# A retention layer and two expert layers on one core: decay masks made by scans instead of copied by transfers

## The chip, the cores and the metric

One Trainium2 chip, one core of it. The metric is the device time of one execution in microseconds (us): 525.28 us before the change, the median of three runs (523.79 to 527.53).

## The reference, cut to what matters

The program has three parts. The first is a retention layer ("attention" below) over q, k, v of shape 2 x 8 heads x 768 positions x 64, with one decay lam per head:

```python
Dmask = np.where(rel >= 0, lam[:, None, None] ** rel[None, :, :], 0.0)   # rel = i - j
intra = np.einsum('bhic,bhjc->bhij', qb, kb) * Dmask[None]
inter = np.einsum('bhid,bhde->bhie', qb * lam_pow[None], kv_state)       # lam_pow = lam ** (i + 1)
kb_dec = kb * rev_pow[None]                                              # rev_pow = lam ** (block - 1 - j)
kv_state = lam_block * kv_state + np.einsum('bhsd,bhse->bhde', kb_dec, vb)
```

The second part maps its 1536 x 512 result x to `((x @ w1) * (x @ w2)) @ w3 @ w_out`. The third sends each of the 1536 rows to one of 8 experts (argmax of `x @ w_gate`, at most 384 rows for each expert, in order of rows), computes `relu(x @ w1[e]) @ w2[e]` and scales it by the softmax weight. Results are float32.

## The kernel before, in words

**Stages, in order of time.** Attention (0 to 72 us), the product of w3 and w_out (72 to about 121 us), the gate stage with w1 and w2 and the ranking of rows, then the experts. Products of float32 accuracy are made from high and low parts (`whi`, `wlo`, `xth`, `xtl`) with three matmuls each (L295 to L297).

**Attention** runs over `it` 0 to 7, each one pair of heads of one batch (`pair = it // 2`), in blocks of 128 positions (`NC` = 6) where the reference has 64, which gives the same result. `part1(it)`: GpSimd scales the queries (`qs`, L394); TensorE makes the scores (24 matmuls, L408); VectorE multiplies them with the mask (`at`, L417, four instructions); TensorE makes the keys-by-values of the blocks from decayed keys `kd` (20 matmuls, L430); VectorE carries the state along the blocks with one scan (`state`, L438). `part2(it - 1)` follows in the same iteration: L454 (24 matmuls) and L468 (20), ScalarE and VectorE split the output (L477, L478). Then ScalarE makes `kd` for the next iteration (`decay_keys`, L379).

**Masks before.** VectorE makes powers of lam by doubling (L334, L337) in `tab`, whose row for a head is 127 zeros, a one, and the powers. ScalarE copies the powers to `lp`. A mask of 128 x 128 is copied from one row of `tab`, each partition reading 128 elements that start one element later (`load_mask`, L356, two transfers of 64 KB for each pair, on the SP queue). That order of partitions reverses positions in a block, so the host reverses keys and values in blocks. TensorE turns powers into a column (`kcol`, L372) that scales the keys.

**Loads.** The SP queue issues in program order: `tqk` and `tkv` of an iteration (L306, L308), then staged weights (`st`, L122). `tqk` has two buffers, `tkv` three; `load_qkv(it + 2)` stands at the end of iteration `it`, so an issue waits until its buffer's readers are through, and what is behind it on the queue waits too. Weights w_out and w3 come in chunks of 512 KB as 64-bit floats; a piece of one is turned to float32 by ScalarE (L132, L133, L142), VectorE (L135, L138) and GpSimd (L143). `TICKS` says where in an iteration a piece begins: one in `it` 1, two in each later one, the second at its end. Chunks 0 to 7 are w_out, chunk 8 and on w3; a staging buffer comes free when the chunk four places earlier has been read by VectorE.

**Keeping TensorE running.** `keep_warm(n)` issues n matmuls on zeros (L325): `WARM` = 15 at the start, `KW` = (7, 6) in iteration 0 after the scores and after the keys-by-values.

```python
def keep_warm(count):
    for _ in range(count):
        nc.tensor.matmul(wacc, warm[:, 0:P], warm, start=True, stop=True)
```

Of the kernel before, what the change touches and what calls it, by code (L numbers as in the profile page):

```python
# [8 lines left out]
F32 = mybir.dt.float32  # L9
F32R = mybir.dt.float32r  # L10
F16 = mybir.dt.float16
# [17 lines left out]
BIG = 1 << 20  # L29
WARM = 15  # L30
KW = (7, 6)
NST = 4
# [8 lines left out]
@with_exitstack  # L41
def tile_moe_chain(ctx, tc, cap, qk, kv, lamb, w12, w3i, woi, wgi, e1i, e2i, c32, c16, zero, out):
    nc = tc.nc
# [20 lines left out]
    def bank():  # L64
        return ps.tile([P, 512], F32, tag="b", name="bank")
# [138 lines left out]
    def run_bg(n=1):  # L204
        for _ in range(n):
            feed.tick()
# [62 lines left out]

    c32_sb = const.tile([P, 156], F32, name="c32_sb")  # L270
    c16_sb = const.tile([P, 256 + ntab], F16, name="c16_sb")
# [4 lines left out]
    utri = c16_sb[:, 0:128]  # L276
    ones = c16_sb[:, 128:256]
    iota = c16_sb[:, 256 : 256 + ntab]
    csum = const.tile([P, NE], F16, name="csum")
# [20 lines left out]
    with pool("att", 2, side="right") as ap, pool("att1", side="right") as a1:  # L300
# [3 lines left out]
        def load_qkv(it):  # L304
            tqk = ap.tile([P, 2, S], F32, tag="qk", name="tqk")
            nc.sync.dma_start(tqk, qk[it])  # L306
            tkv = ap.tile([P, 2, NC, P], F32, tag="kv", name="tkv", bufs=3)
            nc.sync.dma_start(tkv, kv[it])  # L308
            loads[it] = (tqk, tkv)

        tab = ring.tile([P, 2080], F32, tag="1l", name="tab")[:, 0:1024]
        tab = tab.rearrange("p (a n) -> p a n", n=256)
        lp = a1.tile([P, 4, P], F32, name="lp")
        decay = a1.tile([P, 2, (NC - 1) * 64], F32, name="decay")
        lam_sb = a1.tile([P, 4], F32, name="lam_sb")
# [10 lines left out]

        keep_warm(WARM)
        nc.vector.memset(wg_sb, 0.0)
        nc.gpsimd.memset(tab[:, :, 0:127], 0.0)
        nc.gpsimd.memset(tab[:, :, 127:128], 1.0)  # L330
        nc.gpsimd.memset(decay, 0.0)
        states = [a1.tile([P, (NC - 1) * 64], F32, name=f"state{n}") for n in range(2)]
        pw = tab[:, :, 128:256]
        nc.vector.tensor_copy(pw[:, :, 0:1], lam_sb.rearrange("p (a b) -> p a b", b=1))  # L334
        n = 1
        while n < P:
            nc.vector.tensor_tensor(  # L337
                pw[:, :, n : 2 * n],
                pw[:, :, 0:n],
                pw[:, :, n - 1 : n].to_broadcast([P, 4, n]),  # L340
                op=ALU.mult,
            )
            n *= 2
        nc.scalar.copy(lp, pw)

        def set_decay(pair):
            r = lp[:, pair, 127:128]
# [19 lines left out]
        kcol = a1.tile([P, 2, 4], F32, name="kcol")  # L367
        for h in range(2):
            kp = bank()[:, 0:4]
            for k in range(4):  # L370
                row = tab[h * 64 : h * 64 + 1, k, 127:255]
                nc.tensor.matmul(kp[:, k : k + 1], row, row[:, 0:1], start=True, stop=True)  # L372
            nc.vector.tensor_copy(kcol[:, h, :], kp)
# [14 lines left out]
        def part1(it, ticks):  # L388
            pair = it // 2
            if it % 2 == 0:  # L390
# [5 lines left out]
                tqk[:, 0, :].rearrange("p (c i) -> p c i", i=P),  # L396
                bass.AP(lp.tensor, lp[:, pair, :].offset, [lp[:, pair, :].ap[0], [0, NC], [1, P]]),
                op=ALU.mult,
# [3 lines left out]
            for half in range(2):  # L402
                sc = [bank(), bank()]
                for c in range(3):
                    cc = half * 3 + c
                    for h in range(2):
                        hs = slice(h * 64, h * 64 + 64)
                        nc.tensor.matmul(  # L408
                            sc[h][:, c * P : (c + 1) * P],
                            tqk[hs, 1, cc * P : (cc + 1) * P],  # L410
                            tqk[hs, 0, cc * P : (cc + 1) * P],
                            start=True,
                            stop=True,
                        )
                for h in range(2):
                    m = dmask[:, 2 * pair + h, :]
# [68 lines left out]
        for it in range(8):  # L485
# [75 lines left out]
    p2 = late.enter_context(pool("p2", 2, side="right"))  # L561
    enabled.update(w12_it)
    gts = {}
    tabs = psi.tile([P, 512], F32, tag="i", name="tabs")[:, 0 : nch * NE]
# [439 lines left out]
```

## Time and profile before

| | before |
|---|---|
| median of three runs | 525.28 us |
| the profiled execution's own time | 528.52 us |
| its span in the profile | 526.7 us |
| TensorE, matmuls busy | 507.0 us (96%) |
| VectorE busy | 263.5 us (50%) |
| ScalarE busy | 243.7 us (46%) |
| GpSimd busy | 129.4 us (25%) |
| bytes moved by transfers | 81.28 MB, mean 154 GB/s |

PE is TensorE's matmul side, PEld its weight loads, DVE VectorE, ACT ScalarE, POOL GpSimd, SP the engine whose queue issues most transfers; a q behind a name is that engine's sequencer. Shares of the whole span mix the stages: in the first 58 us the transfer engines are busy nearly all the time, after that they are not. TensorE's matmuls are pipelined, so that a busy stretch is not one at its peak.

### The profile page before, as it was taken

What the parts mean: (1) busy time and instruction counts of PE and PEld (TensorE: products, weight loads), DVE (VectorE), ACT (ScalarE), POOL (GpSimd) and SP (SyncE); (2) the same over time, 40 slices, a digit from 0 to 9 for tenths busy, and PEclk for the clock granted to TensorE, in tenths of its full rate; (3) what the DMA queues carried; (4) which work ended last, traced back from release to release, by engine and by line L of the source; (5) the groups of instructions that cost most, each with busy time, mean ns of one, the idle gap of its engine ahead of it and who ended that gap; (6) DMA issues with size and microseconds to landing.
All of it is one profiled execution on the core that took longest, in us unless ns stands there. A gap on an engine that the chain in (4) does not pass through costs nothing. (4 is left out here: it accounts for less than half of the span.)

```text
span 526.7 us, 9643 instructions
## 1 busy us (share of the span) xinstructions
PE 507.0 (96%) x3833; PEld 473.8 (90%) x3833; DVE 263.5 (50%) x572; ACT 243.7 (46%) x487; POOL 129.4 (25%) x126
## 2 busy tenths in 40 slices
PE   9889799999999999999999999899999999999994
PEld 4778699999899999999999999889898998989893
DVE  3597757565643222322233364476574747466420
ACT  2488569676831122112211342367574646466410
POOL 2255436443511000000002003603333240400101
PEclk9999899999999999999999999999999999999998
DMA  7999637555582000000010033557856666674300
GB/s 240 392 369 359 221 120 249 195 184 175 183 284 84 31 0 1 32 30 1 1 42 21 1 119 112 182 190 250 296 182 208 219 221 211 221 240 153 117 1 34
DMA packets 26210, 81.28 MB, mean 154 GB/s; under 512 B 4426, under 2 KB 7372, under 8 KB 26160
## 3 DMA queue, kind: packets, MB, share of 16 engines
q1 hardware_dynamic: 20128, 70.79, 39.2%
q0 software_dynamic: 3344, 7.85, 4.7%
q10 hardware_dynamic: 2688, 1.97, 1.1%
q8 instruction: 32, 0.52, 0.4%
q14 instruction: 18, 0.15, 0.1%
HBM read 74.78 MB, written 10.54 MB: 162 GB/s over the span
## 5 line engine op out<-in xcount | busy, mean ns | idle before, releaser
L97 DVE TENSOR_TENSOR wlo<-st,whi 128x512 fp32r<-128x512 f32 x128 | 82.0, 685 | 15.2 <-ACT whi L95 15.2
L295 PE MATMUL bank<-xtl,whi 128*128 128x384 f32 x256 | 87.2, 341 | 1.1 <-DVE t L138 1.1
L297 PE MATMUL bank<-xth,wlo 128*128 128x384 f32 x256 | 86.4, 338 | 0.0
L296 PE MATMUL bank<-xth,whi 128*128 128x384 f32 x256 | 85.9, 336 | 0.0
L95 ACT CAST whi<-st 128x512 fp32r<-128x512 f32 x128 | 72.9, 621 | 16.7 <-PE bank L297 9.4
L800 PE MATMUL bank<-xdl,whi 128*128 128x256 f32 x256 | 72.6, 284 | 2.2 <-issue 1.7
L800 PE MATMUL bank<-xdh,wlo 128*128 128x256 f32 x256 | 72.1, 282 | 0.0
L800 PE MATMUL bank<-xdh,whi 128*128 128x256 f32 x256 | 72.0, 281 | 0.0
L143 POOL TENSOR_TENSOR wlo<-t,whi 128x512 fp32r<-128x512 f32 x40 | 51.8, 1296 | 67.1 <-ACT whi L142 51.5
L295 PE MATMUL bank<-wxl,gh 128*128 128x264 f32 (+1 forms) x192 | 55.9, 291 | 0.0
L296 PE MATMUL bank<-wxh,gh 128*128 128x264 f32 (+1 forms) x192 | 54.1, 282 | 0.0
L297 PE MATMUL bank<-wxh,gl 128*128 128x264 f32 (+1 forms) x192 | 54.1, 282 | 0.0
L579 DVE TENSOR_TENSOR a_sb<-bank,a_sb 128x384 f32<-128x384 f32 x32 | 17.8, 558 | 68.3 <-PE bank L297 64.1
L800 PEld LDWEIGHTS bank<-xdl,whi 128*128 128x128 f32 x256 | 48.4, 189 | 3.1 <-issue 2.0
L295 PE MATMUL bank<-wlo,hh 128*128 128x512 f32 x128 | 50.8, 397 | 0.0
L297 PE MATMUL bank<-whi,hl 128*128 128x512 f32 x128 | 50.3, 393 | 0.0
L296 PE MATMUL bank<-whi,hh 128*128 128x512 f32 x128 | 50.3, 393 | 0.0
L295 PEld LDWEIGHTS bank<-xtl,whi 128*128 128x128 f32 x256 | 48.1, 188 | 1.7 <-DVE t L138 1.1
L813 DVE SCALAR_TENSOR_TENSOR hl<-bank,hh 128x512 fp32r<-128x512 f32 x32 | 22.1, 691 | 53.4 <-ACT hh L812 43.8
L731 POOL DMA_INDIRECT out_dram<-y,idx x16 | 16.1, 1006 | 132.3 <-ACT y L932 113.1
L800 PEld LDWEIGHTS bank<-xdh,whi 128*128 128x128 f32 x256 | 48.3, 189 | 0.3
L800 PEld LDWEIGHTS bank<-xdh,wlo 128*128 128x128 f32 x256 | 48.3, 189 | 0.0
(114 smaller groups left out, 1018.0 us busy)
## 6 DMA issues: line engine op xcount, KB each, us to landing
st<-e1i SPq DMA_DIRECT2D x32, 512.0 KB
st<-e2i SPq DMA_DIRECT2D x32, 512.0 KB
st<-w3i SPq DMA_DIRECT2D x16, 512.0 KB
st<-w SPq DMA_DIRECT2D x16, 512.0 KB
tqk<-qk SPq DMA_DIRECT2D x8, 768.0 KB
tkv<-kv SPq DMA_DIRECT2D x8, 768.0 KB
st<-woi SPq DMA_DIRECT2D x8, 512.0 KB
out_dram<-zero SPq DMA_DIRECT2D x1, 3072.0 KB
```

The lines of the kernel that those rows point to most:

```text
L95: nc.scalar.copy(h, s)
L97: nc.vector.tensor_tensor(lo, s, h.bitcast(F32), op=ALU.subtract)
L143: nc.gpsimd.tensor_tensor(lo, t, h.bitcast(F32), op=ALU.subtract)
L295: nc.tensor.matmul(acc, wh, rl, start=first, stop=False)
L296: nc.tensor.matmul(acc, wh, rh, start=False, stop=False)
L297: nc.tensor.matmul(acc, wl, rh, start=False, stop=last)
L579: nc.vector.tensor_tensor(a_sb, accs[1], a_sb, op=ALU.mult)
L731: nc.gpsimd.indirect_dma_start(out=out, out_offset=bass.IndirectOffsetOnAxis(ap=idx[:, col : col + 1], axis=0), in_=src, in_offset=None, b ...
L800: nc.tensor.matmul(o, w[:, k, :], x[:, k, :], start=m == 0 and k == 2 and x is xl, stop=m == 1 and k == 1 and w is lo, skip_group_check=True,)
L813: nc.vector.scalar_tensor_tensor(hl, acc, 0.0, hh.bitcast(F32), op0=ALU.max, op1=ALU.subtract)
```

## The change: what it does

- Masks and powers of one pair of heads are made by VectorE with three scans of 128 x 128 (`make_pair`): two whose added operand is the identity matrix give the masks of the two heads, `mask[j, i] = lam * mask[j, i - 1] + (i == j)`, and one gives the powers. Pair 0 at the start, the next ones at the end of iterations 0, 2 and 4.
- Masks and powers are held for two pairs, not four. `tab`, `kcol`, the eight mask transfers and the reversal on the host are gone; the last column of a mask scales the keys.
- `tqk` has three buffers. Loads of iteration 1 and the first chunk are issued before anything else on SP but the constants `c32` (identity, 78 KB before, 84.5 KB now), which were loaded by ScalarE's queue in iteration 1.
- `wgi` is padded to 64 KB by the host and loaded at the end of iteration 2 (16 KB at the end of iteration 1 before, into a zeroed tile). The ranking constants `c16` are loaded in the gate stage, after gate unit (0, 3), not in iteration 4.
- `WARM` is 12 and `KW` is (0, 4).

```diff
-WARM = 15
-KW = (7, 6)
+WARM = 12
+KW = (0, 4)
...
-            tqk = ap.tile([P, 2, S], F32, tag="qk", name="tqk")
+            tqk = ap.tile([P, 2, S], F32, tag="qk", name="tqk", bufs=3)
...
-        lp = a1.tile([P, 4, P], F32, name="lp")
+        lp = a1.tile([P, 2, P], F32, name="lp")
-        dmask = a1.tile([P, NE, P], F32, name="dmask")
-        nc.sync.dma_start(lam_sb, lamb)
+        dmask = a1.tile([P, 4, P], F32, name="dmask")
+        nc.sync.dma_start(c32_sb, c32)
         load_qkv(0)
+        load_qkv(1)
+        feed.load(1)
...
-        while n < P:
-            nc.vector.tensor_tensor(
-                pw[:, :, n : 2 * n],
-                pw[:, :, 0:n],
-                pw[:, :, n - 1 : n].to_broadcast([P, 4, n]),
-                op=ALU.mult,
-            )
-            n *= 2
-        nc.scalar.copy(lp, pw)
+        def powers(out, lam, add, first):
+            nc.vector.tensor_tensor_scan(
+                out, lam.to_broadcast([P, P]), add, first, op0=ALU.mult, op1=ALU.add
+            )
+
+        def make_pair(pair):
+            for e in range(2 * pair, 2 * pair + 2):
+                powers(dmask[:, e % 4, :], lam8[:, e : e + 1], ident, 0.0)
+            none = c32_sb[:, 168:169].to_broadcast([P, P])
+            powers(lp[:, pair % 2, :], lam2[:, pair : pair + 1], none, 1.0)
+
+        make_pair(0)
...
-        def load_mask(pair):
-            for h2 in range(2):
-                r = tab[h2 * 64 : h2 * 64 + 1, pair, 0:1]
-                nc.sync.dma_start(
-                    dmask[:, 2 * pair + h2, :],
-                    bass.AP(r.tensor, r.offset, [[r.ap[0][0], 1], [1, P], [1, P]]),
-                )
-
-        load_mask(0)
-        load_qkv(1)
-        feed.load(1)
...
-                    scale=kcol[:, h, it // 2 : it // 2 + 1],
+                    scale=dmask[:, (it // 2 * 2 + h) % 4, P - 1 : P],
...
-            if it in (0, 1, 3):
-                load_mask((it + 3) // 2)
-            if it == 1:
-                nc.scalar.dma_start(c32_sb, c32)
-                nc.scalar.dma_start(wg_sb[:, :, 0:NE], wgi)
-            if it == 4:
-                nc.scalar.dma_start(c16_sb, c16)
+            if it in (0, 2, 4):
+                make_pair(it // 2 + 1)
+            if it == 2:
+                nc.scalar.dma_start(wg_sb, wgi)
...
+        if (g, fb) == (0, 3):
+            nc.scalar.dma_start(c16_sb, c16)
```

## Rows read from the trace of the kernel before

**Rows 1.** Stretches: us, busy us of each engine, TensorE's granted clock, transfer share, GB/s

```profile
2.00:58.00 56.00, 51.64 (x681) 40.21 (x679) 37.98 (x75) 30.55 (x60) 24.05 (x19) 1.00 0.98 353
7.00:13.00 6.00, 6.00 (x71) 4.33 (x70) 2.59 (x7) 1.04 (x2) 0.87 (x1) 1.00 0.89 254
14.00:24.00 10.00, 8.29 (x137) 7.16 (x138) 4.72 (x9) 4.21 (x9) 3.04 (x3) 1.00 1.03 406
24.00:36.00 12.00, 10.45 (x158) 9.20 (x156) 11.77 (x22) 9.24 (x19) 4.31 (x3) 1.00 1.00 353
36.00:48.00 12.00, 11.94 (x190) 9.93 (x189) 10.49 (x19) 11.04 (x22) 8.31 (x7) 1.00 1.00 388
62.00:68.00 6.00, 6.00 (x64) 4.63 (x62) 4.04 (x8) 3.76 (x7) 4.30 (x3) 0.50 0.52 158
72.00:160.00 88.00, 86.89 (x621) 86.27 (x620) 53.92 (x93) 61.03 (x119) 37.72 (x29) 1.00 0.62 208
```

**Rows 2.** Timeline of all engines, iteration 7: start, duration, instruction, idle before it

```profile
56.93 0.48 PE L408 MATMUL bank<-tqk 64*128 64x128 f32 x2
58.06 0.62 ACT L132 ACTIVATE bank<-st 128x512 f32<-128x512 f32 x1 [5.28 <-DMA st<-w3i]
60.26 0.95 PE L408 MATMUL bank<-tqk 64*128 64x128 f32 x12 [2.84 <-DVE xtl L478]
61.43 1.65 PE L408 MATMUL bank<-tqk 64*128 64x128 f32 x10 [0.22 <-ACT wt L220]
67.84 1.45 PE L468 MATMUL bank<-qs,state 64*64 64x128 f32 x20
...
72.02 0.39 PE L295 MATMUL bank<-wlo,whi 128*128 128x256 f32 x1
```

**Rows 3.** The same view, iteration 4

```profile
35.73 0.93 PE L408 MATMUL bank<-tqk 64*128 64x128 f32 x10 [0.65 <-ACT wt L220]
...
39.20 1.40 PE L468 MATMUL bank<-qs,state 64*64 64x128 f32 x20
```

**Rows 4.** Timeline of the SP queue: issues, start and duration

```profile
4.55 1.22 SPq L356 DMA_DIRECT2D dmask<-tab  x2
5.81 0.59 SPq L306 DMA_DIRECT2D tqk<-qk  x1
...
47.44 0.33 SPq L306 DMA_DIRECT2D tqk<-qk  x1
47.86 0.38 SPq L308 DMA_DIRECT2D tkv<-kv  x1
48.41 41.96 SPq L122 DMA_DIRECT2D st<-w3i  x15
```

**Rows 5.** Timeline of all engines, iterations 0 to 2

```profile
1.19 6.10 PE L325 MATMUL bank<-warm 128*128 128x512 f16 x15 [1.19 <-DVE warm L320]
2.40 0.17 DVE L334 COPY tab<-lam_sb 128x4 f32<-128x4 f32 x1 [1.13 <-DMA lam_sb<-lamb]
6.07 1.80 POOL L394 TENSOR_TENSOR qs<-tqk,lp 128x768 f32<-128x768 f32 x1 [0.42 <-DMA tqk<-qk]
8.68 1.61 PE L408 MATMUL bank<-tqk 64*128 64x128 f32 x24
10.22 1.69 PE L325 MATMUL bank<-warm 128*128 128x512 f16 x7
13.08 1.80 POOL L394 TENSOR_TENSOR qs<-tqk,lp 128x768 f32<-128x768 f32 x1 [5.21 <-DMA tqk<-qk]
21.62 0.56 ACT L379 ACTIVATE kd<-tkv,kcol 128x320 f32<-128x320 f32 x1 [1.57 <-DMA tkv<-kv]
23.17 1.95 DVE L417 TENSOR_TENSOR at<-bank,dmask 128x384 f32<-128x384 f32 x4 [2.54 <-DMA dmask<-tab]
```

**Rows 6.** One line's instructions (L438, then L337): durations, ns, least/median/most

```profile
L438 DVE TENSOR_TENSOR_SCAN state<-decay,bank x8: 812/816/821, 12.8 to 65.4; 128x320 f32<-128x320 f32 x8
...
L337 DVE TENSOR_TENSOR tab<-tab x7: 167/191/424, 2.6 to 4.0; 128x4 f32<-128x4 f32 x1, 128x8 f32<-128x8 f32 x1, 128x16 f32<-128x16 f32 x1, 128x32 f32<-128x32 f32 x1
```

**Rows 7.** Waits of TensorE, 72 to 160 us: total, times, longest

```profile
PE bank L295 <- DVE t L138: 1.1, 2, 0.8
```

More of the change, by code (lines that the diff above doesn't have):

```diff
@@ L41, in tile_moe_chain @@
 @with_exitstack
-def tile_moe_chain(ctx, tc, cap, qk, kv, lamb, w12, w3i, woi, wgi, e1i, e2i, c32, c16, zero, out):
+def tile_moe_chain(ctx, tc, cap, qk, kv, w12, w3i, woi, wgi, e1i, e2i, c32, c16, zero, out):
     nc = tc.nc
@@ L268, in tile_moe_chain @@
         (e1_it, e2_it)[w][2 * e + j] = it
-    c32_sb = const.tile([P, 156], F32, name="c32_sb")
-    c16_sb = const.tile([P, 256 + ntab], F16, name="c16_sb")
+    c32_sb = const.tile([P, 169], F32, name="c32_sb")
     ident = c32_sb[:, 0:128]
@@ L275, in tile_moe_chain @@
     gsum = c32_sb[:, 148:156]
-    utri = c16_sb[:, 0:128]
-    ones = c16_sb[:, 128:256]
-    iota = c16_sb[:, 256 : 256 + ntab]
+    lam2 = c32_sb[:, 156:160]
+    lam8 = c32_sb[:, 160:168]
     csum = const.tile([P, NE], F16, name="csum")
@@ L327, in tile_moe_chain @@
         keep_warm(WARM)
-        nc.vector.memset(wg_sb, 0.0)
-        nc.gpsimd.memset(tab[:, :, 0:127], 0.0)
-        nc.gpsimd.memset(tab[:, :, 127:128], 1.0)
         nc.gpsimd.memset(decay, 0.0)
         states = [a1.tile([P, (NC - 1) * 64], F32, name=f"state{n}") for n in range(2)]
-        pw = tab[:, :, 128:256]
-        nc.vector.tensor_copy(pw[:, :, 0:1], lam_sb.rearrange("p (a b) -> p a b", b=1))
-        n = 1
-        while n < P:
-            nc.vector.tensor_tensor(
-                pw[:, :, n : 2 * n],
-                pw[:, :, 0:n],
-                pw[:, :, n - 1 : n].to_broadcast([P, 4, n]),
-                op=ALU.mult,
-            )
-            n *= 2
-        nc.scalar.copy(lp, pw)
+        def powers(out, lam, add, first):
+            nc.vector.tensor_tensor_scan(
+                out, lam.to_broadcast([P, P]), add, first, op0=ALU.mult, op1=ALU.add
+            )
+        def make_pair(pair):
[4 more added lines that the diff above has]
+        make_pair(0)
         def set_decay(pair):
-            r = lp[:, pair, 127:128]
+            r = lp[:, pair % 2, 127:128]
             nc.gpsimd.tensor_copy(
@@ L351, in set_decay @@
             )
-        def load_mask(pair):
-            for h2 in range(2):
-                r = tab[h2 * 64 : h2 * 64 + 1, pair, 0:1]
-                nc.sync.dma_start(
-                    dmask[:, 2 * pair + h2, :],
-                    bass.AP(r.tensor, r.offset, [[r.ap[0][0], 1], [1, P], [1, P]]),
-                )
-        load_mask(0)
-        load_qkv(1)
-        feed.load(1)
         nc.vector.memset(csum, 0.0)
         enabled.update(wo_it + w3_it[:2])
[L367 to L373, printed above, removed]
         kds = {}
@@ L396, in part1 @@
                 tqk[:, 0, :].rearrange("p (c i) -> p c i", i=P),
-                bass.AP(lp.tensor, lp[:, pair, :].offset, [lp[:, pair, :].ap[0], [0, NC], [1, P]]),
+                bass.AP(lp.tensor, lp[:, pair % 2, :].offset, [lp.ap[0], [0, NC], [1, P]]),
                 op=ALU.mult,
@@ L415, in part1 @@
                 for h in range(2):
-                    m = dmask[:, 2 * pair + h, :]
+                    m = dmask[:, (2 * pair + h) % 4, :]
                     nc.vector.tensor_tensor(
@@ L562, in tile_moe_chain @@
     enabled.update(w12_it)
+    c16_sb = p2.tile([P, 256 + ntab], F16, name="c16_sb", bufs=1)
+    utri = c16_sb[:, 0:128]
+    ones = c16_sb[:, 128:256]
+    iota = c16_sb[:, 256 : 256 + ntab]
     gts = {}
@@ L945 @@
     q, k, v, lam = f("q"), f("k"), f("v"), f("lam")
-    def rev(a):
-        return a.reshape(2, 8, NC, P, 64)[:, :, :, ::-1].reshape(2, 8, S, 64)
     def tr(a):
@@ L954, in nat @@
         return a.reshape(2, 4, 2, NC, P, 64).transpose(1, 0, 4, 3, 2, 5).reshape(8, P, NC, P)
-    kr, vr = rev(k), rev(v)
     w1, w2, w3, wo = f("moe_w1"), f("moe_w2"), f("moe_w3"), f("moe_w_out")
@@ L967 @@
     nch = min(-(-cap // P), NBLK)
-    c32 = np.zeros((P, 156), np.float32)
+    c32 = np.zeros((P, 169), np.float32)
     c32[:, 0:128] = np.eye(P)
@@ L975 @@
     c16[:, 256:] = np.arange(nch * P)
+    c32[:, 156:160] = np.repeat(lam.reshape(4, 2).T, 64, axis=0)
+    c32[:, 160:168] = lam
+    wgi = np.zeros((P, 4, 32), np.float32)
+    wgi[:, :, 0:NE] = f("moe2_w_gate").reshape(4, P, NE).transpose(1, 0, 2)
     w1h, w2h = kfb(w1), kfb(w2)
     arrays = {
-        "qk": np.stack([tr(q), tr(kr)], 2),
-        "kv": np.stack([nat(kr), nat(vr)], 2),
-        "lamb": np.repeat(lam.reshape(4, 2).T, 64, axis=0),
+        "qk": np.stack([tr(q), tr(k)], 2),
+        "kv": np.stack([nat(k), nat(v)], 2),
         "w12": np.stack([w1h[0], w2h[0], w1h[1], w2h[1]]),
@@ L983 @@
         "woi": wo.reshape(2, 4, P, DM).transpose(0, 2, 1, 3).reshape(2, P, 2048),
-        "wgi": f("moe2_w_gate").reshape(4, P, NE).transpose(1, 0, 2),
+        "wgi": wgi,
         "e1i": np.stack([kfb(e1[e]) for e in range(NE)]),
```

3 lines of the change are left out of this document (removed).

## The prediction

> **What bounds the kernel now.** I read the stretches first, since the chain of waits starts only near the end of the span. From 2 to 58 us the transfer engines are busy 0.98 of the time [rows 1]; after that transfers have slack. From 72 us on TensorE has almost no gap (86.89 of 88 us busy to 160 us), so what the change can win lies before 72 us, and moves the later stages forward as a whole.
>
> Within attention there are three regimes. In iterations 0 to 2 data is late: the second queries are seen at 13.08 us after 5.21 us of idle GpSimd, and VectorE waits 2.54 us for a mask transfer at 23.17 us [rows 5]. From 24 to 36 us VectorE is busy 11.77 of 12 us and sets the pace; from 36 to 48 us TensorE, ScalarE and VectorE are all nearly full (11.94, 11.04, 10.49) [rows 1]. In iteration 6 data is late again: ScalarE stands 5.28 us until chunk 9 of the weights (the second of w3) lands at 58.06 us; behind it stand the output copies of part2(5), VectorE's subtraction, a PSUM bank, and TensorE, idle 2.84 us up to 60.26 us [rows 2]. TensorE's granted clock, full until then, is 0.50 from 62 to 68 us [rows 1], the lower of its two levels: what it did before it fell was to stand those 2.84 us.
>
> **The change part by part.**
>
> *Start.* Gone are the doubling chain (seven instructions of 191 ns median [rows 6]), the ScalarE copy, the column matmuls and the first mask transfers, which cannot be issued until 4.55 us and stand ahead of the second tqk on SP, issued at 5.81 us [rows 4]. Now SP issues constants, both pairs of loads and a chunk back to back. The constants take the place of lam, seen at 2.40 us [rows 5], and being 84.5 KB come some 0.5 us later, so pair 0's scans run from about 3.0 us.
>
> A scan of 128 x 128: the trace has one shape, 128x320 in 816 ns [rows 6]. In proportion to its elements it would be 0.33 us, and at most the whole 0.82 us. I take 0.40 us, near the first, as the row is mostly elements: three make 1.2 us for a pair (1.0 to 2.45). Pair 0 is ready by 4.3 us, before the first scores.
>
> From 7 to 13 us the transfers move 254 GB/s while busy 0.89, against 406 GB/s in the stretch from 14 to 24 us [rows 1]: the two masks' rows stand between large ones, and the hole is worth 6 x (1 - 254/406) = 2.2 us. At 406 GB/s the second tqk, a third transfer of 768 KB after one seen at 6.07 us [rows 5], follows two more such transfers of 1.94 us each: about 10.2 us for 13.08. Later ones gain more, for the masks and the constants are no longer among them: the third tqk about 15.5 us, its tkv about 17.4 us, where ScalarE saw it at 21.62 us [rows 5].
>
> The Trainium skill speaks against so large a gain (DMA: Bandwidth & Descriptors, "Why small descriptors are slow (HBM only)"): it holds that transfers from SBUF to SBUF, as the masks are, do not suffer from small packets and keep 78% of the link's best rate. By it a pair of masks would cost an estimated 0.4 us, the hole would be no work of theirs, and the sum below would be some 2 us smaller. The row with 254 GB/s at a share of 0.89 speaks for the masks; the measurement decides.
>
> TensorE: three of 15 warm matmuls go, at 6.10/15 = 0.41 us each, and seven of 1.69 us in all after the first scores [rows 5]; two of the six after the keys-by-values go. Twelve end at about 6.2 us, when the first tqk lands, so the scores begin at 6.4 instead of 8.68 us. Keys-by-values then wait for tkv and ScalarE until about 9.3 us; the second scores come at about 11, the third at 17.4. VectorE begins the third iteration's masks at about 18.3 instead of 23.17 us: **-4.9 us**. Bounds: -2.3 (only the first scores' lead holds) and -5.5.
>
> *Scans later.* Pair 1's stand at the end of iteration 0 on an idle VectorE: nothing. If that cover is gone, 1.2 us. Pair 2's stand at the end of iteration 2, where VectorE sets the pace: +1.2 us, behind them a weight piece and the masks of iteration 3, for which TensorE's next part2 waits. Pair 3's fall in the stretch where VectorE has 1.5 of 12 us free [rows 1]: between 0 and 1.2, I take +0.6. Together **+1.8 us** (1.0 to 4.9).
>
> *Data just in time.* With VectorE 4.9 us earlier, chunks 2 and 3 and the fourth tkv land within half a microsecond of their use: **+0.5 us** (0 to 1.5). So the middle of the stage runs about 2.6 us ahead.
>
> *Third query buffer, chunk 9.* Today the last tqk waits for its buffer until 47.44 us, the last tkv goes at 47.86 and chunk 9 at 48.41 [rows 4]. With three buffers tqk waits for nothing recent; tkv (three buffers as before) still waits for part2(4), so chunk 9 is issued at about 45. Ahead of its end lie 16 transfers of 768 KB, ten of 512 KB and 0.15 MB of constants, 18.0 MB, from 2 us on. At 406 GB/s with 1.2 us for the slow first two microseconds they end at 47.5, at 388 [rows 1] at 49.6, and are seen 1 to 3 us after that. TensorE's wait of 2.84 us is gone if chunk 9 lands by 58.06 - 2.84 - 2.6 = 52.6 us. It does, with little to spare: **-2.8 us** (0 to -2.8).
>
> *Clock.* Without that idle the clock should stay up. Price: from the last ten score matmuls to L468 it takes 67.84 - 61.43 = 6.41 us at the low level and 39.20 - 35.73 = 3.47 us at the full one [rows 2, 3]: **-2.9 us** (0 to -2.9).
>
> *Moved and dropped.* The c16 load costs one issue of ScalarE in the gate stage, where ScalarE is busy 61.03 of 88 us [rows 1] and ranking needs it much later: nothing; 0.4 us without that cover. wgi is issued an iteration later and needed some 9 us after that: nothing, or up to 1 us of TensorE if late. Eight issues of 0.6 us leave SP, which stands behind busy transfers anyway.
>
> **Sum:** -4.9 + 1.8 + 0.5 - 2.8 - 2.9 = -8.3 us. Against the profiled execution, 528.52 us (1.8 of it outside the span), that is 520.2. That execution is 3.24 us above the median, about the price of the clock's fall, and the runs do not tell whether the median one had it. If it had, 525.28 - 8.3 = 517.0; if not, the gain is 5.4 and the time 519.9. I take **518.0 us**, nearer the first.
>
> **Rivals.**
>
> *Chunk 9 still late.* If the transfers keep their mean of 353 GB/s [rows 1], the 18.0 MB end at 54.1 us, and with 1 us more chunk 9 lands at about 55. For it: 24 to 36 us shows 353 with few masks in it. Against it: 10 us at 406. All before then is swallowed; what remains is 58.06 - 55 = 3 us, with the clock falling as before: 522.3 us. The Trainium skill (DMA: Bandwidth & Descriptors, "Where 436 GB/s comes from") puts the memory limit of a core at about 358 GB/s, which would make this the case; 406 GB/s over 10 us shows more.
>
> *Gain lost behind attention.* The w3 stage lives on prepared pieces, and TensorE waits for VectorE there, though only 1.1 us in two waits [rows 7]. If preparation, not TensorE, were the limit, nothing would arrive at the end: about 525. Against it: ScalarE and VectorE have 27 and 34 us free in those 88 [rows 1], and the pieces move forward with the matmuls.
>
> *Cold start, slower.* Fifteen warm matmuls run 0.41 us apart, seven later ones 0.24 [rows 5]: the rise comes with the end of the first series. With twelve, and no fill between scores and keys-by-values, TensorE could go on at the lower level. An iteration has 5.3 us of matmuls (1.6 + 0.8 + 1.5 + 1.4), and the low level makes them 6.41/3.47 = 1.85 as long: 4.5 us each. After two such iterations the gain is gone; with three, up to about 27 us, the time is 517.0 + 13.5 = 530.5. Against it: the scores follow the twelve at once. The Trainium skill (TensorE: Matmul & The Clock Gate, "What's actually happening") says that low is the resting state and activity lifts it, which leaves this open.
>
> *It does not do what it says.* If SP is held by full transfers and not by buffers, the third query buffer moves nothing; chunk 9 then goes at about 46.5 and still lands by 52.6: inside the forecast's range.
>
> **How the numbers follow.** A change under 1% (5.25 us) can hardly be told from none here. Forecast 0.55 (518.0, its own range 514 to 520); chunk 9 late 0.20 (522.3, a quarter of it under 520.0 if the clock holds); lost behind 0.10 (525); cold start 0.07 (530.5); scans at the dear end 0.08 (-8.3 + 3.1 = -5.2: 520.1, half under 520.0). Faster: 0.55 + 0.05 + 0.04 = 0.64, less 0.02 for the forecast's own upper end: 0.62. Same: 0.31. Slower: 0.07. Low end: 517.0 less 0.8 for cheap scans, 0.6 for the larger lead and about 1.5 for the spread of runs: 514. High end: the late chunk with that spread: 524.
>
> **What would show it.** Right: masks of iteration 2 near 18.3 us; no transfer rate near 254 GB/s before 13 us; scans near 0.4 us; chunk 9 landing by 52.6 us; no TensorE gap near 2.8 us in iteration 7; granted clock 1.00 through 72 us; the first L295 near 64 us instead of 72.02 [rows 2]. Wrong: a ScalarE wait for w3 that stays, a clock of 0.50 before 30 us, or a first L295 at 64 with the span unmoved.

## The result, and the profile after

The changed kernel takes 520.76 us, the median of 12 runs (518.09 to 522.96), beside 525.70 us for the kernel before, the median of 12 runs in the same comparison (523.62 to 529.02). The ratio is 0.9902, its 95% interval 0.9877 to 0.9927: by it 0.98% less, at the edge of what the forecast called no change. In two later comparisons, each on a chip of its own, it was 0.9903 (0.9874 to 0.9933) and 0.9878 (0.9857 to 0.9900). The profiled execution takes 520.25 us, with a span of 518.4 us.

Stretches of the kernel after, the columns as in [rows 1]:

```profile
7.00:13.00 6.00, 4.31 (x66) 3.25 (x62) 4.10 (x9) 3.31 (x5) 2.60 (x3) 1.00 1.01 413
14.00:24.00 10.00, 9.10 (x156) 8.20 (x152) 8.61 (x18) 6.17 (x13) 1.83 (x1) 1.00 1.02 407
24.00:36.00 12.00, 10.30 (x168) 8.93 (x168) 10.92 (x20) 10.18 (x20) 8.04 (x7) 1.00 1.02 412
36.00:48.00 12.00, 11.49 (x172) 9.69 (x170) 10.20 (x22) 11.28 (x23) 7.21 (x7) 1.00 1.01 390
62.00:68.00 6.00, 6.00 (x53) 6.00 (x52) 4.01 (x8) 3.78 (x10) 2.15 (x3) 1.00 0.53 164
331.00:341.00 10.00, 10.00 (x64) 9.51 (x65) 6.95 (x13) 6.71 (x13) 1.16 (x1) 0.86 0.38 129
```

The hole of 254 GB/s is filled (413), and 353 GB/s from 24 to 36 us became 412; the granted clock from 62 to 68 us is 1.00 where it was 0.50 [rows 1]. The last row is new: at the start of the expert stage the clock is 0.86.

Timeline of the kernel after (start, duration, instruction, idle before it):

```profile
2.73 0.74 DVE L329 TENSOR_TENSOR_SCAN dmask<-c_sb 128x128 f32<-128x128 f32 x2 [1.59 <-DMA c_sb<-c]
3.38 0.40 DVE L329 TENSOR_TENSOR_SCAN lp<-c_sb 128x128 f32<-128x128 f32 x1
6.32 1.61 PE L385 MATMUL bank<-tqk 64*128 64x128 f32 x24
7.59 1.28 ACT L356 ACT_TABLE_LOAD   x1 [7.59 <-DMA tkv<-kv]
9.47 1.81 POOL L371 TENSOR_TENSOR qs<-tqk,lp 128x768 f32<-128x768 f32 x1 [1.99 <-DMA tqk<-qk]
9.50 1.25 PE L407 MATMUL bank<-tkv,kd 128*64 128x64 f32 x20 [1.56 <-ACT kd L356]
17.66 1.94 DVE L394 TENSOR_TENSOR at<-bank,dmask 128x384 f32<-128x384 f32 x4
23.07 0.56 ACT L356 ACTIVATE kd<-tkv,dmask 128x320 f32<-128x320 f32 x1 [0.97 <-DMA tkv<-kv]
23.25 0.40 DVE L329 TENSOR_TENSOR_SCAN lp<-c_sb 128x128 f32<-128x128 f32 x1
25.06 0.80 PE L407 MATMUL bank<-tkv,kd 128*64 128x64 f32 x20 [1.96 <-DVE t L138]
...
42.24 28.85 SPq L122 DMA_DIRECT2D st<-w3i  x11
48.69 0.66 ACT L132 ACTIVATE bank<-st 128x512 f32<-128x512 f32 x1 [0.95 <-DMA st<-w3i]
51.91 1.94 PE L385 MATMUL bank<-tqk 64*128 64x128 f32 x24
...
60.53 0.39 PE L293 MATMUL bank<-wlo,whi 128*128 128x256 f32 x1
...
318.08 0.37 ACT L629 COPY rowa<-bank 128x256 f32<-128x256 f32 x1
329.38 0.58 ACT L762 CAST xdh<-bank 128x512 fp32r<-128x512 f32 x1 [5.26 <-remote]
330.75 0.58 PE L780 MATMUL bank<-xdl,whi 128*128 128x256 f32 x1 [2.65 <-issue]
```

These rows answer to [rows 2, 4, 5]: L385 is L408 of before, L371 L394, L356 L379, L394 L417, L407 L430, L293 L295. VectorE's masks of iteration 2 begin at 17.66 us for 23.17, without a wait; chunk 9 is seen at 48.69 us for 58.06, after 0.95 us of waiting for 5.28; the last scores begin at 51.91 us for 56.93, with no gap ahead of them. The first product of w3 comes 11.5 us earlier, at 60.53 for 72.02 us. The span is only 8.3 us shorter: the gap in front of the first expert (L780) and the low clock after it give back 3.2 us. The copy of rows and the cast ahead of that gap in the kernel before, 10.07 us apart where they are now 11.30, and below them the first entry of its ScalarE:

```profile
329.66 0.37 ACT L651 COPY rowa<-bank 128x256 f32<-128x256 f32 x1
339.73 0.58 ACT L782 CAST xdh<-bank 128x512 fp32r<-128x512 f32 x1 [4.00 <-PE bank L770]
...
0.73 1.28 ACT L344 ACT_TABLE_LOAD   x1 [0.73 <-PEq L994]
```

### The profile page after: what moved, and what is told of

The parts are those of the page before. It is cut to its first block, busy times and chain, and to the rows that moved or that the text cites. A ratio compares the mean times of both kernels' runs of the same rounds, so it can differ in the third digit from the quotient of the medians.

```text
span 518.4 us, 9565 instructions
## 1 busy us (share of the span) xinstructions
PE 499.3 (96%) x3805; PEld 469.4 (91%) x3805; DVE 264.1 (51%) x573; ACT 243.0 (47%) x486; POOL 128.8 (25%) x124
## 5 line engine op out<-in xcount | busy, mean ns | idle before, releaser
L293 PE MATMUL bank<-xtl,whi 128*128 128x384 f32 x256 | 87.3, 341 | 1.4 <-DVE t L138 1.4
L295 PE MATMUL bank<-xth,wlo 128*128 128x384 f32 x256 | 86.4, 337 | 0.0
L780 PE MATMUL bank<-xdl,whi 128*128 128x256 f32 x256 | 73.3, 286 | 3.7 <-issue 2.6
L780 PE MATMUL bank<-xdh,whi 128*128 128x256 f32 x256 | 72.8, 284 | 0.0
L780 PE MATMUL bank<-xdh,wlo 128*128 128x256 f32 x256 | 72.6, 284 | 0.0
L293 PE MATMUL bank<-wxl,gh 128*128 128x264 f32 (+1 forms) x192 | 55.9, 291 | 0.0
L295 PE MATMUL bank<-wxh,gl 128*128 128x264 f32 (+1 forms) x192 | 54.1, 282 | 0.0
L780 PEld LDWEIGHTS bank<-xdl,whi 128*128 128x128 f32 x256 | 49.1, 192 | 4.6 <-issue 2.8
L557 DVE TENSOR_TENSOR a_sb<-bank,a_sb 128x384 f32<-128x384 f32 x32 | 17.8, 557 | 68.0 <-PE bank L295 63.7
L293 PE MATMUL bank<-wlo,hh 128*128 128x512 f32 x128 | 51.1, 399 | 0.0
L711 POOL DMA_INDIRECT out_dram<-y,idx x16 | 17.3, 1082 | 135.1 <-ACT y L912 100.0
L295 PE MATMUL bank<-whi,hl 128*128 128x512 f32 x128 | 50.4, 394 | 0.0
L293 PEld LDWEIGHTS bank<-xtl,whi 128*128 128x128 f32 x256 | 48.1, 188 | 2.0 <-DVE t L138 1.4
L780 PEld LDWEIGHTS bank<-xdh,whi 128*128 128x128 f32 x256 | 49.0, 191 | 0.3
L780 PEld LDWEIGHTS bank<-xdh,wlo 128*128 128x128 f32 x256 | 49.0, 192 | 0.0
```

The costliest lines, as they stand in the source:

```text
L293: nc.tensor.matmul(acc, wh, rl, start=first, stop=False)
L295: nc.tensor.matmul(acc, wl, rh, start=False, stop=last)
L557: nc.vector.tensor_tensor(a_sb, accs[1], a_sb, op=ALU.mult)
L711: nc.gpsimd.indirect_dma_start(out=out, out_offset=bass.IndirectOffsetOnAxis(ap=idx[:, col : col + 1], axis=0), in_=src, in_offset=None, b ...
L780: nc.tensor.matmul(o, w[:, k, :], x[:, k, :], start=m == 0 and k == 2 and x is xl, stop=m == 1 and k == 1 and w is lo, skip_group_check=True,)
```

## The experiments

Three sets, each on one chip of its own beside runs of the kernel before. "First product" is the start of the first w3 matmul, "rest" the span less that.

| | median us | ratio (95%) | profiled: span | first product | rest |
|---|---|---|---|---|---|
| *first chip*: before again | 525.50 | 1.0003 (0.9971 to 1.0035) | 523.5 | 68.49 | 455.0 |
| after again | 520.29 | 0.9903 (0.9874 to 0.9933) | 518.4 | 60.37 | 458.0 |
| after + row transfers | 521.85 | 0.9932 (0.9907 to 0.9957) | 520.0 | 62.64 | 457.4 |
| after, scans doubled | 525.20 | 0.9996 (0.9966 to 1.0026) | 526.2 | 68.07 | 458.1 |
| *second chip*: before + early loads | 520.83 | 0.9983 (0.9965 to 1.0001) | 517.6 | 64.11 | 453.5 |
| after, two query buffers | 517.28 | 0.9924 (0.9900 to 0.9949) | 515.2 | 61.18 | 454.0 |
| after, pair 2's scans late | 519.98 | 0.9960 (0.9928 to 0.9992) | 516.6 | 62.45 | 454.2 |
| after, three pairs early | 515.64 | 0.9877 (0.9846 to 0.9908) | 513.9 | 60.38 | 453.5 |
| *third chip*: before again | 523.26 | 1.0019 (0.9989 to 1.0049) | 519.7 | 66.11 | 453.6 |
| after again | 516.28 | 0.9878 (0.9857 to 0.9900) | 515.1 | 61.55 | 453.6 |
| three pairs early again | 515.40 | 0.9860 (0.9839 to 0.9881) | 513.8 | 60.45 | 453.4 |
| after, warm matmuls of before | 516.80 | 0.9894 (0.9873 to 0.9916) | 514.9 | 60.85 | 454.1 |

**The kernel before again, on two chips** (no edit). Does the stall in iteration 6, with the clock's fall after it, belong to every execution?

> The kernel before, unchanged, profiled once more. If the clock's fall at 61 us belongs to some executions only (theory): TensorE still idles 2 to 3 us near 57 to 60 us, but the granted clock stays 1.00 from 60 to 70 us, the first w3 product (L295) starts at about 69 instead of 72.0 us and the span is about 523.8 us. If it belongs to every execution (rival): granted clock 0.50 from 62 to 68 us again and a span of 526 to 527 us; then the median's gain of 5 us hides 3 us lost somewhere later.

> The kernel before, a third profile, beside the next three on one chip. Theory (chunk 9's landing is what varies from execution to execution): ScalarE waits 3 to 5.5 us for it again, TensorE idles 1 to 3 us in iteration 7, first w3 product 66 to 72 us; from the last row copy of the gate stage to the end of the span 196 to 197.5 us, as in the changed kernels of the same chip.

First chip: ScalarE's wait for chunk 9, the last scores, and two stretches:

```profile
55.98 0.63 ACT L132 ACTIVATE bank<-st 128x512 f32<-128x512 f32 x1 [3.72 <-DMA st<-w3i]
58.19 0.95 PE L408 MATMUL bank<-tqk 64*128 64x128 f32 x12 [1.28 <-DVE xtl L478]
...
59.00:63.00 4.00, 3.78 (x44) 2.60 (x42) 3.79 (x8) 3.40 (x7) 2.61 (x2) 0.57 0.42 120
62.00:68.00 6.00, 6.00 (x102) 5.54 (x104) 4.02 (x7) 4.94 (x10) 3.81 (x3) 0.93 0.44 149
```

Third chip, the same:

```profile
55.09 0.65 ACT L132 ACTIVATE bank<-st 128x512 f32<-128x512 f32 x1 [2.07 <-DMA st<-w3i]
57.19 1.16 PE L408 MATMUL bank<-tqk 64*128 64x128 f32 x14
...
62.00:68.00 6.00, 6.00 (x82) 5.59 (x81) 5.38 (x9) 5.80 (x12) 4.44 (x4) 1.00 0.48 135
```

Three executions of one kernel: ScalarE waits 5.28, 3.72 and 2.07 us, TensorE stands 2.84, 1.28 and 0 us, the clock from 62 to 68 us is 0.50, 0.93 and 1.00, and the first product comes at 72.02, 68.49 and 66.11 us. On the first chip the clock did fall, only earlier and for less long: it is 0.57 from 59 to 63 us. So neither expectation held as written: on the first chip the stall was shorter than the theory's 2 to 3 us and the clock fell all the same, and on the third ScalarE waited less than 3 us and TensorE not at all. The stall is real and its size is not fixed; the execution from which the prediction was made had it at its largest. What belongs to the chip and what to the single execution is not told apart by three profiles, but the twelve runs on the first chip alone lie between 522.74 and 529.57 us. The profiled run there, 525.28 us, is close to their median; the one on the third, 521.45 us, is 1.8 us under its median.

**The kernel after again, on two chips** (no edit). Do the 3 us at the experts belong to the change?

> The changed kernel, unchanged, profiled once more. Both theories: first w3 product within 0.5 us of 60.5 us, ratio to before 0.988 to 0.993. Theory (the wait where the experts begin is chance): TensorE's gap near 330 us differs from 2.65 us by 0.5 us or more and the clock there may stay full, span 516.5 to 519. Rival (the change moved a load into that place): again 2.6 us and a fall of the clock, span 518.4 within 0.5 us.

> The changed kernel, a third profile. First w3 product 60 to 61 us on any chip. If the 3 us that it lost after attention in two profiles belong to the change (rival), 200 us from the last row copy to the end and a fall of the clock near 330 us again, ratio to before 0.990; if they belong to the chip and the moment (theory), 196 to 197.5 us, and a ratio of 0.986 to 0.990.

First chip; the gap and the low clock come back:

```profile
330.79 0.58 PE L780 MATMUL bank<-xdl,whi 128*128 128x256 f32 x1 [2.60 <-issue]
...
330.00:336.00 6.00, 5.21 (x32) 5.21 (x33) 2.90 (x5) 2.78 (x7) 1.91 (x2) 0.72 0.10 30
```

Third chip:

```profile
24.00:30.00 6.00, 4.79 (x62) 4.50 (x64) 4.96 (x9) 3.75 (x8) 4.31 (x3) 0.72 1.03 411
...
319.19 0.37 ACT L629 COPY rowa<-bank 128x256 f32<-128x256 f32 x1
327.83 0.59 ACT L762 CAST xdh<-bank 128x512 fp32r<-128x512 f32 x1 [2.58 <-PE bank L750]
...
330.00:342.00 12.00, 12.00 (x77) 10.84 (x76) 9.79 (x16) 8.12 (x16) 1.62 (x2) 1.00 0.65 204
```

On the third chip TensorE has no gap there (12.00 of 12 us) and the clock stays at 1.00. From the last row copy to the first cast it takes 8.64 us; the kernel before takes 8.63 there (323.64 to 332.27 us). In the first comparison and on the first chip the same stretch takes 10.07 and 10.29 us before, 11.30 and 11.26 after. On the first chip the rival held to the letter (gap 2.60 us, span 518.4 us); the third chip decides that the 3 us are no fixed price of the change: the rest of the program is as long for both kernels on the third chip (453.6 us; 196.1 and 195.9 us from that copy to the end), and 3 us longer for the changed one on the first. That the gathers land later on the first chip, and another microsecond later in the changed kernel, is measured; why is **open**. Two things narrow it. The doubled scans below bring the first product of that chip back to 68.07 us, as late as in the kernel before, and their rest is still 458.1 us, so an earlier arrival alone does not explain it. And GpSimd stands 1.3 to 1.5 us ahead of the same gather (L701 of the kernel after) in every profile of a changed kernel with the longer rest, and 0.3 us in the others. The move of the `c16` load into the gate stage was not undone in any run. On the third chip another disturbance showed, a clock of 0.72 from 24 to 30 us, and the gain of the profiled pair is 4.6 us, in the first product and in the span alike; by the medians it is 6.3 us there.

**The masks' transfers back, without their use.** Six copies of rows, two at each place of the later masks, into a tile that nothing reads (`copy_rows`, not shown, issues two transfers of 64 KB: 128 rows of 512 bytes out of one partition). The first pair's two, in front of the loads of iteration 1, are not put back:

```diff
+            if it in (0, 1, 3):
+                copy_rows(0)
```

> The changed kernel with six transfers of 64 KB put back on the SP queue where iterations 0, 1 and 3 issued mask transfers, of the same form (each partition reads 128 elements of one row, one element further), into a tile that nobody reads. Theory (such transfers cost the engines far more than their bytes): the transfer rate shows holes as before, chunk 9's wait on ScalarE grows from 0.95 to 2.5 to 4 us, first w3 product 2 to 4 us later (62.5 to 64.5). Rival (they cost their bytes only, 0.39 MB at 406 GB/s = 1 us): first w3 product 0 to 0.7 us later.

```profile
51.59 0.66 ACT L132 ACTIVATE bank<-st 128x512 f32<-128x512 f32 x1 [2.03 <-DMA st<-w3i]
...
24.00:36.00 12.00, 9.51 (x156) 8.19 (x158) 10.21 (x19) 10.12 (x20) 7.25 (x6) 1.00 1.01 384
```

Chunk 9 is seen 2.26 us later than in the kernel after on that chip (49.33 us), the first product 2.27 us later, the median 1.56 us. From 24 to 36 us the rate is 384 GB/s for 408. The transfers hold 0.39 MB, 1.0 us at 406 GB/s; in this pair of executions they cost more than twice that, and by the medians half as much again. The forecast of 2 to 4 us for the first product held; the hole in the rate (the lowest stretch is 384 GB/s) and a wait of 2.5 us or more did not come. This is the direct measurement of six of the eight mask transfers: about three tenths of the change's gain on that chip. Whether the engines or the queue pay is not told apart, for each two issues also hold the SP queue 1.1 to 2.3 us, and chunk 9 is issued 1.0 us later (43.02 for 42.02 us).

**Scans doubled** after the first pair:

```diff
             if it in (0, 2, 4):
                 make_pair(it // 2 + 1)
+                make_pair(it // 2 + 1)
```

> The changed kernel with the three scans made twice at the end of iterations 0, 2 and 4 (1.1 us more of VectorE each time). Theory (VectorE sets the pace in iterations 2 and 3, less so in 4 and 5): first w3 product 2.0 to 2.8 us later (+1.1 after iteration 2, +0.6 after iteration 4, +0.3 to 1.1 after iteration 0). Rival (the scans lie beside other work): 0 to 0.4 us later.

```profile
11.00:14.00 3.00, 3.00 (x18) 1.84 (x18) 2.70 (x7) 1.01 (x2) 0.66 (x2) 0.51 1.02 390
...
25.31 1.75 DVE L329 TENSOR_TENSOR_SCAN dmask<-c_sb 128x128 f32<-128x128 f32 x2
25.33 1.44 POOL L143 TENSOR_TENSOR wlo<-t,whi 128x512 fp32r<-128x512 f32 x1 [4.97 <-ACT whi L142]
26.73 1.92 POOL L371 TENSOR_TENSOR qs<-tqk,lp 128x768 f32<-128x768 f32 x1
26.98 1.95 DVE L329 TENSOR_TENSOR_SCAN lp<-c_sb 128x128 f32<-128x128 f32 x1
30.34 1.34 PE L407 MATMUL bank<-tkv,kd 128*64 128x64 f32 x20 [5.49 <-issue]
...
24.00:36.00 12.00, 6.51 (x82) 5.90 (x79) 10.33 (x17) 4.71 (x10) 4.61 (x3) 0.72 0.82 316
```

The median is 4.9 us above the kernel after, more than the scans' own time: nine more of 0.40 us are 3.6 us. The profiled execution (528.01 us) is 2.8 us above that median, so its first product, 7.7 us later than the kernel after's and outside both expectations, is not the median's price. Alone a scan takes 0.40 us; beside GpSimd the second mask and the powers take 1.4 and 1.95. Each ends 0.3 us after the GpSimd instruction that began before it (26.77 and 28.65 us; the scans end at 27.06 and 28.93). TensorE then stands 5.49 us where it stood 1.96 us, and its clock, 0.72 over the stretch, adds to it. Of the 7.7 us, 1.8 are there before these scans begin: the clock is 0.51 from 11 to 14 us, after TensorE stood 2.22 us up to 9.64 us, ahead of the keys-by-values, and the scores of iteration 1 take 2.59 us for 1.61. The first extra scans begin only at 12.67 us; this start is the change's own.

The Trainium skill (SBUF — State Buffer, "SBUF: two separate sides") describes this: VectorE and GpSimd share a pair of ports as an exclusive lock, taken also by a VectorE instruction with two SBUF inputs against a GpSimd instruction that reads SBUF, and whoever starts first keeps it for the whole instruction. The trace agrees, with those two ends. In the kernel after all 12 scans take 0.40 us (the longest 0.42), since GpSimd happens to be idle beside every one.

**The early order of loads alone**, in the kernel before: the second pair of loads and the first chunk ahead of the first masks, as the change has them.

```diff
         load_qkv(0)
+        load_qkv(1)
+        feed.load(1)
...
         load_mask(0)
-        load_qkv(1)
-        feed.load(1)
```

> The kernel before with one thing of the change: loads of iteration 1 and the first chunk are issued ahead of the first mask transfers. Theory (early order needs masks that come by no transfer): the second tqk lands near 10 us instead of 13, but the first masks now stand behind 2 MB and land near 13 us, so the first mask products start 3 to 4 us later than 9.6 us; first w3 product between 67.5 and 71, ratio 0.996 to 1.003. Rival (the order alone is the gain): first w3 product 3 us or more ahead of the kernel before (65.5 or less), ratio 0.994 or less.

```profile
7.00:13.00 6.00, 6.00 (x70) 4.12 (x70) 0.33 (x2) 2.04 (x4) 2.69 (x3) 1.00 1.04 378
...
13.07 1.95 DVE L417 TENSOR_TENSOR at<-bank,dmask 128x384 f32<-128x384 f32 x4 [4.85 <-DMA dmask<-tab]
```

The masks come at 13.07 us, behind the larger transfers, and VectorE waits 4.85 us for them. By the ratio the time is 0.17% lower, in an interval that reaches 1: the theory's range. The first product of the profiled execution is the rival's: 64.11 us, 2.0 us ahead of the earliest of the three executions of the kernel before (none of them on this chip), but that execution was the fastest of its twelve, 519.41 us for a median of 520.83. The interval leaves the order alone 0.35% at most, about a third of the change's gain. From 7 to 13 us the rate is 378 GB/s, with the first masks on their way, where the kernel before has 254 to 269: most of that hole goes with the order. That the rest needs masks that don't travel is argued; no run has the one without the other for the first pair.

**Two query buffers** in the kernel after:

```diff
-            tqk = ap.tile([P, 2, S], F32, tag="qk", name="tqk", bufs=3)
+            tqk = ap.tile([P, 2, S], F32, tag="qk", name="tqk")
```

> The changed kernel with two buffers for tqk instead of three. Theory (the engines' bytes are the limit and tkv's buffer holds the queue anyway): chunk 9 is issued about 1 us later, first w3 product 0 to 0.8 us later, ratio to before 0.989 to 0.992. Rival (the third buffer carries the end of the stall): chunk 9 lands 3 us later, TensorE idles 1 us or more in iteration 7, first w3 product 2 us or more later.

```profile
42.93 8.10 SPq L122 DMA_DIRECT2D st<-w3i  x4
...
50.13 0.67 ACT L132 ACTIVATE bank<-st 128x512 f32<-128x512 f32 x1 [2.47 <-DMA st<-w3i]
```

Chunk 9 is issued at 42.93 us for 42.24, since the last tkv holds the queue until 41.8 us even with three buffers, and is seen at 50.13 us for 48.69. TensorE has no gap. The first product comes at 61.18 us, beside 60.53, 60.37 and 61.55 us in the three executions of the kernel after: so by these profiles the third buffer is worth 0 to 0.8 us, as the theory had it. Chunk 9 comes forward because the loads ahead of it do, and hardly by the buffer.

**Pair 2's scans behind the weight piece** at the end of iteration 2:

```diff
-            if it in (0, 2, 4):
+            if it in (0, 4):
                 make_pair(it // 2 + 1)
...
+            if it == 2:
+                make_pair(2)
```

> The changed kernel with pair 2's three scans moved behind the weight piece that begins at the end of iteration 2, where GpSimd is at work (L143 and the scaling of queries); nothing is added or removed. Theory (a scan on SBUF operands runs several times slower while GpSimd works, as in the doubled run where one took 1.95 us instead of 0.40): the three scans take 3 to 5 us instead of 1.1, first w3 product 2 to 4 us later. Rival (the long scans of the doubled run had another cause): 1.1 us as before, first w3 product within 0.4 us.

```profile
24.72 1.28 POOL L143 TENSOR_TENSOR wlo<-t,whi 128x512 fp32r<-128x512 f32 x1 [5.91 <-ACT whi L142]
24.78 1.50 DVE L329 TENSOR_TENSOR_SCAN lp<-c_sb 128x128 f32<-128x128 f32 x1
25.96 1.95 POOL L371 TENSOR_TENSOR qs<-tqk,lp 128x768 f32<-128x768 f32 x1
26.78 1.62 PE L431 MATMUL bank<-at,tkv 128*64 128x128 f32 x16 [1.67 <-DVE at L394]
```

One scan meets GpSimd and takes 1.50 us, ending at 26.28 us, again 0.3 us after the GpSimd instruction ahead of it (26.00 us). The three take 2.2 us for 1.1, less than the 3 to 5 that were expected. TensorE waits 1.67 us for VectorE's masks and the clock falls behind it (0.86 from 24 to 36 us, as in the kernel after on the third chip); the first product is 0.9 to 2.1 us later than in those three executions. The wait for GpSimd is shown; its price is not. The median is 2.7 us above that of the kernel with two query buffers on the same chip, but the twelve runs are two groups, six from 516.2 to 518.4 us and six from 521.5 to 522.6; the profiled one, 518.42 us, is of the lower group, which overlaps the runs of that kernel (516.21 to 522.56). What the upper group does, no profile shows.

**Masks of three pairs made at the start**, kept in a buffer that is free during attention, and one ScalarE copy at the start, so that its table is loaded before the keys land:

```diff
-            if it in (0, 2, 4):
-                make_pair(it // 2 + 1)
+            if it == 4:
+                make_pair(3)
...
-        make_pair(0)
+        for pair in range(3):
+            make_pair(pair)
...
+        pre = a1.tile([P, 1], F32, name="pre")
+        nc.scalar.copy(pre, warm[:, 0:1])
```

> The changed kernel with the scans of pairs 0, 1 and 2 all at the start, on idle VectorE and GpSimd (two pairs held in a weight buffer that is free until iteration 5), and with one small ScalarE copy at the start, so that the 1.28 us load of its activation table does not stand behind the first tkv at 7.6 us. Theory (VectorE and the table load are on the path): keys-by-values of iteration 0 at 8.2 instead of 9.5 us, first w3 product 1 to 2.5 us earlier (58 to 59.5), ratio 0.985 to 0.989. Rival (data landing is the limit already): waits for tkv and for chunk 9 grow by what is saved, first w3 product within 0.5 us, ratio 0.990.

> Scans of three pairs at the start and the early table load, beside the changed kernel on one chip. Theory (transfers are the limit from iteration 2 on): first w3 product within 0.5 us of the changed kernel, median 0 to 1 us below it. Rival (VectorE was still on the path): 1.5 us or more below it.

On the second chip:

```profile
0.74 1.28 ACT L330 ACT_TABLE_LOAD   x1 [0.74 <-PEq L981]
...
8.34 1.25 PE L415 MATMUL bank<-tkv,kd 128*64 128x64 f32 x20 [0.94 <-ACT kd L364]
```

On the third:

```profile
23.05 0.56 ACT L364 ACTIVATE kd<-tkv,masks 128x320 f32<-128x320 f32 x1 [1.18 <-DMA tkv<-kv]
48.86 0.67 ACT L132 ACTIVATE bank<-st 128x512 f32<-128x512 f32 x1 [1.21 <-DMA st<-w3i]
```

Keys-by-values come at 8.34 us for 9.50, yet the keys of iteration 3 are used at 23.05 us as before (23.07): what was won waits for the transfers, which were full already. Chunk 9 is seen at 48.86 us and the first product at 60.4 us, no earlier than in the changed kernel's best execution (60.37 us). The median is nevertheless 0.88 us below the kernel after on the same chip, and the first product 1.1 us earlier than there (61.55 us, with the clock's dip at 24 to 30 us, which this kernel doesn't show). It is the fastest version measured, 0.9860 (0.9839 to 0.9881) of the kernel before. Which of its two edits brings that was not run apart. The first product of 58 to 59.5 us that was expected of VectorE and the table load did not come, which speaks for the landing of data as the limit.

**The warm matmuls of before** in the kernel after:

```diff
-WARM = 12
-KW = (0, 4)
+WARM = 15
+KW = (7, 6)
```

> The changed kernel with the old 15 warm matmuls at the start and 7 and 6 in iteration 0. Theory (data decides from iteration 1 on): first scores 0.4 to 1.3 us later, first w3 product within 0.5 us, same time within 0.2%. Rival (TensorE's start is on the path): first w3 product 1 us or more later.

516.80 for 516.28 us, ranges that overlap (516.56 to 517.89; 515.74 to 517.09). The scores begin at 7.26 us for 5.82, and the first product comes at 60.85 us for 61.55, in a comparison with an execution that has the clock's dip. Fewer warm matmuls neither cost nor bring anything that can be told.

## Why the prediction was right or wrong

The time is inside the range (514 to 524) and 2.8 us above the number. The direction was given as faster by over 1% with 0.62; what came is 0.98% faster, with an interval that holds the 1%, and 1.2% on the third chip.

**Right, by its own marks, in the first execution:**

| step | forecast | measured |
|---|---|---|
| pair 0 ready | 4.3 us | 3.78 us |
| scan of 128 x 128 | 0.40 us | 0.40 us |
| first scores | 6.4 us | 6.32 us |
| second queries | 10.2 us | 9.47 us |
| keys-by-values | 9.3 us | 9.50 us |
| masks of iteration 2 | 18.3 us | 17.66 us |
| chunk 9 seen | by 52.6 us | 48.69 us |
| clock, 62 to 68 us | 1.00 | 1.00 |
| first product of w3 | 64 us | 60.53 us |

The mechanism is the one that the prediction gave: masks that don't travel free the transfer engines, data comes earlier, and the stall for chunk 9 with the clock's fall behind it goes. The row transfers put back show some three tenths of it from the other side; how the rest divides among the first pair's transfers, the order of loads and the powers is not shown, and the hole from 7 to 13 us, which the prediction laid to the masks' rows, goes for the most part with the order alone (378 GB/s). The keys-by-values were right by two errors: the keys landed earlier than thought, and a load of ScalarE's table, 1.28 us, began only then, at 7.59 us, where the kernel before had it at 0.73 us, ahead of a copy of the powers that waited for VectorE until 4.49 us.

**Mis-sized, the middle of the stage.** "So the middle of the stage runs about 2.6 us ahead." Start of the scores by iteration, in the first two profiled executions:

| iteration | 0 | 1 | 2 | 3 | 4 | 5 | 6 | 7 |
|---|---|---|---|---|---|---|---|---|
| before, us | 8.68 | 13.96 | 19.93 | 26.58 | 33.92 | 41.56 | 49.40 | 56.93 |
| after, us | 6.32 | 11.64 | 16.57 | 21.49 | 29.46 | 37.10 | 44.84 | 51.91 |
| lead, us | 2.36 | 2.32 | 3.36 | 5.09 | 4.46 | 4.46 | 4.56 | 5.02 |

The lead of about 5 us was right. But scans later (+1.8) and data just in time (+0.5) took 0.6 us of it, between iterations 3 and 4, and no more. Pair 2's scans (22.60 to 23.65 us) do stand on the path: TensorE waits 1.96 us, to 25.06 us, for VectorE's weight piece behind them. Yet the iteration takes 7.97 us for 7.34 before. Against the profiled execution these terms are 2.4 us too dear (5.0 less 2.6 at the last scores).

**Mis-sized, the stall and the clock.** "TensorE's wait of 2.84 us is gone" and "-2.9 us" for the clock were both taken from one execution. It shows the largest of three stalls; another shows 1.28 us and a clock that is low for about half as long, the third neither. On the first chip the profiled runs of both kernels are close to their medians. There the last scores lead by 4.7 us and the first product by 8.1, so stall and clock gave 3.4 us for the 5.7 of the two terms. The middle, 2.1 us better than its 2.6, hides that: 8.1 us is the sum's 8.3 by two errors. "I take 518.0 us, nearer the first" is the choice that was off: the branch without the fall, 519.9 us by a gain of 5.4, was the nearer one, though not for its reason alone, as the next step took 3 us. The comparison gave 4.9 us; the pairs on the first and third chip 5.7 and 6.3 us (525.99 to 520.29, 522.57 to 516.28, the medians of the runs beside them).

**Failed on one chip, the end.** "Moves the later stages forward as a whole": on the third chip it did, 4.6 us of 4.6. On the first chip 3.0 us of the 8.1 were lost at the first expert, where the sum had nothing: without that loss the gain of that pair, 5.1 us, would have been 8.1. Against the profiled execution the sum came out at 520.2 for 520.25 us measured, but by chance: 3.2 us more lead at the first product than the sum held (63.7 to 60.5 us), and 3.2 us lost later.

**Rivals.** *Chunk 9 late* fell: the four stretches of [rows 1] from 7 to 48 us show 390 to 413 GB/s, and 362 to 412 in the other two executions of the kernel after. The Trainium skill (DMA: Bandwidth & Descriptors, "Where 436 GB/s comes from") has about 358 GB/s as a core's memory limit; the measured rate is above it in each of these stretches. *Lost behind attention* fell: the w3 stage is as full as before (86.62 of 88 us of TensorE from 72 to 160 us). *Cold start* did not come at its price, but not wholly without ground. In one of three executions of the kernel after the clock is 0.72 from 24 to 30 us and 0.50 from 26 to 28, a sign that the prediction had listed against itself; before the fall TensorE had stood 1.95 us for VectorE, a wait that the first execution has too (1.96 us), without a fall. And with the doubled scans, whose start is the change's, the clock is 0.51 from 11 to 14 us, after TensorE stood 2.22 us where the fill between scores and keys-by-values had been (the kernel after on the third chip has the same 2.22 us without a fall). That is much like the rival's mechanism, at a price of 1.8 us for the 13.5 that it named. That the first warm matmuls are slow because the clock has yet to rise, as it argued, the granted clock doesn't show: it is 1.00 from 2 us on [rows 1]. *Scans at the dear end* fell here, by grace of an idle GpSimd; the doubled and the moved scans show that the bound was no idle one. *The third buffer moves nothing* was nearly so.

What spoke against the gain, the Trainium skill on packets between SBUF and SBUF (DMA: Bandwidth & Descriptors, "Why small descriptors are slow (HBM only)"), is not borne out in the profiled pair: there six such transfers cost 2.3 us of the first product, more than twice the 1.0 us of their bytes. The medians, 1.56 us apart, say the same less firmly, and the issues' time on the queue is in both.

## What to carry to other kernels

Before a stall in one profile is priced, take more profiles of the same kernel: a wait at the edge of its cover, and the fall of the clock behind it, come and go between executions, and the median holds only part of both. The same goes for the profile of an experiment: see first where its run stands among the others. A small transfer on a queue that is full can cost more than its bytes, and what an otherwise idle engine can compute in a microsecond is worth computing. Put a VectorE instruction with two SBUF operands where GpSimd is idle, and look at the ends of both to see whether one waits for the other.

## What the runs showed that was not expected

- A scan of 0.40 us takes 1.4 to 1.95 us beside a GpSimd instruction that began before it, and ends about 0.3 us after that instruction.
- Attention moved 362 to 413 GB/s between 7 and 48 us on one core, in three executions of the kernel after.
- ScalarE's table load (1.28 us) began at 7.59 us, when the keys had landed, in the kernel after, and so lay on the path; where its first instruction was a copy it began at 0.73 us (the kernel before, whose copy then waited for VectorE until 4.49 us) and 0.74 us (the small copy at the start). What decides whether it runs ahead of a wait, no run shows.
- Between chips the same stretch, from the last copy of rows to the first cast of gathered rows, takes 8.6 us, or 10.1 to 11.8 us with a gap of TensorE; in the changed kernels, where it takes 11.3 us or more, the clock falls too.
- One edit (the late scans) gave two groups of six runs each, around 517.4 and 522.2 us, and the median fell between them.
